# Splitting the last group of queries of an attention kernel in two, with a seventh buffer of exponentials

## The chip, the cores and the metric

The kernel runs on one core of one Trainium2 chip. The metric is device time in microseconds (us), lower is better. The kernel before takes 885.8 us (median of 3 runs, 884.97 to 886.49); the profiled execution has a span of 884.1 us from the first instruction to the last.

The engines are called by the names that the profile uses: PE (matrix multiply), PEld (its weight loads), DVE (vector), ACT (scalar: exponentials and other activations), POOL (GpSimd), SP (the engine that issues transfers).

## The reference

One sequence of 2048 tokens, width 640, 32 heads of 20. An attention branch and a gated branch share one layer norm.

```python
x = A_x                                   # (1, 2048, 640) bf16
xn = layernorm(x)
qkv = (xn @ wqkv) ...                     # 32 heads of 20
scores = einsum("bhqd,bhkd->bhqk", q, k) * 20 ** -0.5
p = softmax(scores)                       # 32 x 2048 x 2048 exponentials
s = einsum("bhqk,bhkd->bhqd", p, v) ... @ wo
# second branch: layernorm, w1, gelu, shifts by 1 or 2 tokens, w2, residual,
#                layernorm, w3, gelu, w4, residual
g = silu(B(xn, w1, w2, w3, w4))
out = x + s * g
```

## The kernel before

The kernel lays out its own schedule when it is built: it lists tasks with their reads, writes, buffers and wished times (`DUE`), orders them for each engine, and emits them with semaphores. Each engine then carries out its list in order. So a change in a constant of the configuration reorders work everywhere.

The 32 heads are taken four at a time (a *quad*, 8 of them), and the queries 512 at a time (4 of them): 32 *groups*. In a group the 2048 keys are 16 tiles of 128. The usual step for a key tile computes the scores of two heads (two PSUM banks, 128 keys x 1024) and one exponential over them on ACT, so a tile costs two exponentials.

```python
    def score_act(self, b, qc, kt, a, gb=None):
        ...
        hs, sa = self.stile()                       # two PSUM banks
        def fn(e):
            for jj in range(2):                     # two heads
                out = self.bank(hs.slot + jj)
                ...
                for c in range(4):
                    ins = e.matmul(out[32 * c:32 * c + 32, :], self.KT[:, b, 128 * kt + 32 * c:...],
                                   self.QM[:, gb, 2 * a + jj, :], start=True, stop=True, tile_position=(0, 32 * c))   # L1420
        T("pe", ..., acq=("S", hs))
        return self.exp_act(hs, sa)

    def exp_act(self, hs, sa):                      # L1444
        self.T("act", ..., lambda e: e.activation(self.PT[:, hp.slot, :],
               self.psum[:, 512 * hs.slot:512 * hs.slot + 1024], AF.Exp, scale=cfg.scale),
               ..., acq=("PT", hp), rel=hs)
```

`PT` holds the exponentials until PE has multiplied them with the values (L1345): six buffers of 128 x 1024. The products gather in PSUM bank 7 (`PVB`), one bank for all groups.

Part of the exponentials is made on DVE from the bits of an integer. A *block* is two key tiles; of each, two heads go to ACT and two to DVE, so a block costs two exponentials on ACT in place of four. `ND[quad][qc]` is the number of blocks of a group. DVE takes the scores to 16-bit integers (L1471, one for each of the two tiles) and makes four pieces of them (L1371, shared by two blocks where a unit has two); PE multiplies each piece with the values (L1380). The scores of a block need two pairs of banks at once:

```python
            pairs = [(0, [0, 1]), (0, [2, 3])]
            high = [(0, [4, 5]), (0, [5, 6]), (1, [4, 6])]
            pl.kind("W", "B", [(0, [4]), (0, [6]), (1, [5])])          # all other matmuls
            pl.kind("S", "B", pairs + ...)                             # scores for ACT
            pl.kind("SD", "B", [(r + q, x + y) for r, x in pairs for q, y in high]     # scores of a block
                    + ([(3, pairs[0][1] + pairs[1][1]), ...] if self.cfg.FALL else []))
```

At the end of a group DVE empties bank 7 (`normalise`). In the last quad it transposes in blocks of 32 (L1493), takes reciprocals (L1495), multiplies (L1501) and transposes back (L1503) into `On7`. In the last group of all, four tiles of 128 tokens then follow: PE multiplies `On7` with the last rows of `wo` (L1602, two banks of kind S), DVE multiplies with the gate (L1609) and adds the part made earlier (L1650), and the row tile is stored (L1652).

```python
    def finish_qc(self, qc):
        split = qc == cfg.NQC - 1
        ...
        for nl in range(4):
            n = 4 * qc + nl
            sl = n % 2
            if split:
                addend, adda = Sb[:, nl, :], [A("Sb", nl, 0), A("Sb", nl, 1)]
            ...
            if split:
                self.wo_last(n, SB2[:, sl, :], ...)                    # L1602, L1609
            ...
            T("dve", ..., lambda e, ...: e.tensor_tensor(OS[:, sl, :], SB2[:, sl, :], addend, op=ALU.add), ...)    # L1650
            T("sp", C_SP, lambda e, ...: e.dma_start(outv[:, n, :], OS[:, sl, :]), ...)                             # L1652
```

Before the first exponential the kernel loads x, normalises it on DVE, ACT and POOL (`POOLN` names the tiles that POOL scales), transposes it on PE and copies it out of PSUM on DVE or ACT, and projects keys and queries of the first quad. A bound on the scores needs the largest key (L1158, L1164, L1166).

## Time and profile before

| what | value | how to read it |
|---|---|---|
| median time | 885.8 us | three runs, 884.97 to 886.49 |
| span of the profile | 884.1 us | one execution |
| first exponential starts | 35.65 us | timeline of ACT |
| last exponential ends | 873.05 us | started 872.00, 1.05 us long |
| ACT busy | 846.9 us, 96% | overlapping instructions included |
| PE busy | 822.8 us, 93% | matmuls are pipelined, so this is not PE at its peak |
| DVE busy | 716.2 us, 81% | |
| POOL busy | 42.9 us, 5% | nearly all in the first 40 us |
| mean granted PE clock | 0.995 | |

A group of the profile is a line of the kernel with its engine, operation, tile and shape; "idle before" is the time its engine stood still just before these instructions, with the instruction that ended most of it. In a timeline a row can stand for several instructions run one after another, as its count says.

### The profile page before, as it was taken

The page shows a single profiled execution, that of the slowest core. Times are in us where ns is not written, and L with a number is a line of the kernel's source. Part 1 is how long each engine was busy: PE and PEld are TensorE (multiplying, and loading weights), DVE is VectorE, ACT ScalarE, POOL GpSimd, SP SyncE. Part 2 cuts the span into 40 slices and gives each one's busy share as a digit, 9 for nine tenths or more (in the row PEclk, how much of TensorE's full clock was granted, in tenths as well). Part 3 has the DMA queues.
Part 4 walks back from the last instruction along what each step waited for, and adds up shares of the span by engine and source line. Part 5 has one row for each costly group of instructions (what it writes and reads, how often), then busy time and mean ns, then how long its engine had stood idle before and what let it go on. Part 6 is the DMA issues. An engine that isn't in the chain of part 4 may idle for free.

```text
span 884.1 us, 34138 instructions
## 1 busy us (share of the span) xinstructions
PE 822.8 (93%) x15594; PEld 361.9 (41%) x15594; DVE 716.2 (81%) x986; ACT 846.9 (96%) x896; POOL 42.9 (5%) x74
## 2 busy tenths in 40 slices
PE   3899999998999999999999899999999799999996
PEld 2433333333444443433334444443433344444553
DVE  7747797876888889999998657997889794898675
ACT  7799999998999999999999999999999999999994
POOL 9500000000000000000000000000000000010000
PEclk9999999999999999999999999999999999999998
DMA  6002632331210002332122302132221212023322
GB/s 224 10 8 61 137 96 73 95 95 36 52 41 25 26 25 64 90 101 52 47 55 62 113 26 56 54 91 69 56 64 44 70 32 69 24 65 101 114 69 75
DMA packets 86481, 59.01 MB, mean 67 GB/s; under 512 B 53057, under 2 KB 77841, under 8 KB 86337
## 3 DMA queue, kind: packets, MB, share of 16 engines
q1 hardware_dynamic: 86336, 56.82, 23.5%
q8 instruction: 123, 2.02, 0.9%
q14 instruction: 22, 0.17, 0.1%
HBM read 42.10 MB, written 10.63 MB: 60 GB/s over the span
## 4 chain that ended last, share of the span: by engine, by line
ACT 55%; PE 19%; DVE 17%; DMA 5%; POOL 1%; issue 1%; POOLq 0%
ACT arena L1444 53%; PE psum L782 8%; PE psum L1420 6%; DVE arena L1371 5%; DVE arena L1471 4%; DMA arena<-recips 3%; PE psum L1345 2%; PE psum L1388 2%; DMA recips<-arena 2%; PE psum L1380 1%; ACT arena L1809 1%; DVE arena L984 1%; ACT arena L1825 1%; DVE arena L1805 1%; DVE arena L1225 1%
## 5 line engine op out<-in xcount | busy, mean ns | idle before, releaser
L1444 ACT ACTIVATE arena<-psum 128x1024 bf16<-128x1024 f32 x834 | 777.8, 1038 | 14.4 <-PE psum L1420 5.0
L1420 PE MATMUL psum<-arena 128*32 128x512 bf16 x4928 | 375.7, 381 | 8.0 <-ACT arena L1444 6.6
L782 PE MATMUL psum<-arena 128*32 128x320 bf16 (+1 forms) x5952 | 359.8, 333 | 6.8 <-DVE arena L1179 2.8
L1471 DVE TENSOR_SCALAR arena<-psum 128x1024 uint16<-128x1024 f32 (+1 forms) x192 | 231.5, 1206 | 42.1 <-PE psum L1388 41.3
L1371 DVE TENSOR_SCALAR arena<-arena 128x4096 uint16<-128x4096 uint16 (+1 forms) x224 | 231.4, 1059 | 3.6 <-PE psum L1380 2.5
L782 PEld LDWEIGHTS psum<-arena 128*32 128x32 bf16 x5952 | 150.5, 97 | 146.2 <-issue 20.7
L1345 PE MATMUL psum<-arena 128*22 128x512 bf16 x1668 | 161.8, 381 | 1.2 <-DVE arena L1506 0.6
L1420 PEld LDWEIGHTS psum<-arena 128*32 128x32 bf16 x4928 | 104.4, 95 | 137.2 <-ACT arena L1444 95.2
L1380 PE MATMUL psum<-arena 128*22 128x512 bf16 x1520 | 126.5, 380 | 2.5 <-DVE arena L1371 2.2
L1388 PE MATMUL psum<-arena 32*128 32x512 bf16 x816 | 85.4, 384 | 16.6 <-ACT arena L1444 9.7
L1345 PEld LDWEIGHTS psum<-arena 128*22 128x22 bf16 x1668 | 42.5, 92 | 55.8 <-issue 11.8
L1388 PEld LDWEIGHTS psum<-arena 32*128 32x128 bf16 x816 | 21.9, 90 | 102.5 <-ACT arena L1444 81.4
L1380 PEld LDWEIGHTS psum<-arena 128*22 128x22 bf16 x1520 | 35.8, 91 | 44.5 <-issue 9.7
L1805 DVE CAST arena<-psum 128x512 bf16<-128x512 f32 x48 | 32.8, 684 | 8.3 <-PE psum L782 8.1
L1225 DVE CAST arena<-psum 128x512 bf16<-128x512 f32 x40 | 27.3, 682 | 10.9 <-PE psum L782 10.8
L1820 DVE TENSOR_TENSOR arena<-psum,arena 128x320 bf16<-128x320 f32 x32 | 15.6, 486 | 22.0 <-PE psum L782 22.0
L1590 DVE SCALAR_TENSOR_TENSOR arena<-psum,arena 128x320 bf16<-128x320 f32 x32 | 15.6, 489 | 19.0 <-PE psum L782 18.9
L1519 DVE TENSOR_TENSOR arena<-arena 128x512 bf16<-128x512 f32 x28 | 19.2, 686 | 11.5 <-DMA arena<-recips 11.4
L984 DVE BATCH_NORM_STATS2 arena<-arena 128x6 f32<-128x320 bf16 x52 | 23.0, 480 | 2.2 <-DMA arena<-in_A_x_dram 2.2
L1286 DVE CAST arena<-psum 128x320 bf16<-128x320 f32 x32 | 15.4, 488 | 10.9 <-PE psum L782 10.5
L1506 DVE COPY arena<-psum 128x512 f32<-128x512 f32 x28 | 19.2, 685 | 3.5 <-PE psum L1345 2.3
L1089 PE MATMUL psum<-arena 128*32 128x128 bf16 x320 | 8.9, 248 | 13.7 <-DVE arena L999 13.1
(103 smaller groups left out, 283.8 us busy)
## 6 DMA issues: line engine op xcount, KB each, us to landing
arena<-in_B_w_dram SPq DMA_DIRECT2D x48, 160.0 KB, 2.6
arena<-recips SPq DMA_DIRECT2D x28, 256.0 KB
arena<-arena SPq DMA_DIRECT2D x124, 32.0 KB, 1.9
arena<-in_B_w_dram SPq DMA_DIRECT2D x4, 960.0 KB, 6.0
arena<-in_A_x_dram SPq DMA_DIRECT2D x8, 320.0 KB, 5.3
arena<-in_A_x_dram SPq DMA_DIRECT2D x16, 160.0 KB, 2.3
out_dram<-arena SPq DMA_DIRECT2D x16, 160.0 KB, 1.8
heads<-arena SPq DMA_DIRECT2D x112, 20.0 KB
```

The costliest lines, as they stand in the source:

```text
L782: ins = e.matmul(pb[32 * c:32 * c + 32, 0:N], lhsT(k, c), rhs(k, c), start=(k == 0), stop=(stop and k == nk - 1), tile_position=(0, 32 * c))
L984: lambda e, li=li, n=n, hh=hh: e.bn_stats(st[:, li, 6 * hh:6 * hh + 6], xn[:, n, hD * hh:hD * hh + hD]),
L1225: T("dve", c_dve(512), lambda e, h=h, c=c: e.tensor_copy(KS[:, 512 * c:512 * c + 512], self.wbank(h)[:, 0:512]), reads=[wa], writes=[A("KS ...
L1345: ins = e.matmul(pb[32 * i:32 * i + 22, 0:512], VA[:, ql, kts[x // 2], i, :], PT[:, slots[x // 2][0].slot, 512 * (x % 2):512 * (x % 2) + 512],
L1371: T("dve", c_dve(w, "4x"), lambda e, v=v, dst=dst: e.tensor_scalar(dst, U[:, ub, 0:w], 0.5, EXP_B[v], op0=ALU.mult, op1=ALU.add), reads=ha ...
L1380: ins = e.matmul(pb[32 * i:32 * i + 22, 0:512], wv, dst[:, at:at + 512].bitcast(BF16), start=first, stop=final, tile_position=(0, 32 * i))
L1388: return e.matmul(out, self.KT[32 * i:32 * i + 32, b, 128 * kt:128 * kt + 128], self.QT[32 * i:32 * i + 32, b, 512 * qc:512 * qc + 512], s ...
L1420: ins = e.matmul(out[32 * c:32 * c + 32, :], self.KT[:, b, 128 * kt + 32 * c:128 * kt + 32 * c + 32], self.QM[:, gb, 2 * a + jj, :], start ...
L1444: lambda e: e.activation(self.PT[:, hp.slot, :], self.psum[:, 512 * hs.slot:512 * hs.slot + 1024], AF.Exp, scale=cfg.scale),
L1471: ins = e.tensor_scalar(U[:, ub, 1024 * at + 512 * k:1024 * at + 512 * k + w], self.psum[:, 512 * hd.slots[k]:512 * hd.slots[k] + w], a_ex ...
L1506: T("dve", c_dve(512), lambda e: e.tensor_copy(Ob[:, :], self.bank(self.PVB)[:, :]), writes=[("PV", 0), A("Ob")], name=f"ob{quad}_{qc}", c ...
L1805: T("dve", c_dve(512), lambda e, h=h, fc=fc, i=i: e.tensor_copy(GT[:, i, fc, :], self.wbank(h)[:, 0:512]), reads=[wa], writes=at, name=f"g ...
```

## The change

The last group of queries (quad 7, queries 1536 to 2047) is done in two halves of 256 queries. A score tile then holds four heads by 256 queries, and one exponential covers all four heads of a key tile. Each half gathers its products in a bank of kind W of its own, and is normalised on its own, so the first half can go on to the output projection while the second is being computed. Four of the 32 tile-halves go to DVE whole (`LAST`: three in the first half, one in the second), with the scores in a pair of kind S. `PT` has seven buffers in place of six. The last outputs are added in place, so the second pair of tiles doesn't wait for the store of the first. With this comes a new set of the tuned constants: `DUE`, `ND`, `RESERVE`, `POOLN`, `TRA` (which transposed tiles ACT copies out), and `FALL` is off. An unused path (`score_half`, `ROWK`) goes.

```diff
-        self.RESERVE = 1000.0
-        self.POOLN = [1, 9, 13, 15]
+        self.RESERVE = 200.0
+        self.POOLN = [1, 5, 9, 13]
...
-        self.FALL = True
+        self.FALL = False
...
+        self.LNA = [3, 3]
+        self.TRA = [1, 5, 7, 9, 11, 13, 15, 17, 19]
+        self.ONP = 0
+        self.LAST = [[[0, 2], [7, 1]], [[2, 1]]]
         self.ND = (
-            [1, 2, 3, 3],
-            [3, 3, 3, 4],
-            [3, 3, 3, 3],
-            [2, 3, 4, 4],
-            [4, 2, 2, 4],
-            [4, 3, 3, 3],
-            [4, 4, 2, 3],
-            [4, 3, 1, 2])
+            [1, 2, 4, 3],
+            [2, 3, 3, 4],
+            [3, 4, 3, 2],
+            [3, 2, 4, 4],
+            [3, 2, 3, 3],
+            [4, 3, 4, 3],
+            [4, 4, 3, 3],
+            [4, 4, 3, 0])
...
-            pl.pool("PT", 6)
+            pl.pool("PT", 7)
...
-                act = bk % 2 == 1
+                act = bk in cfg.TRA
...
+            if last and qc == NQC - 1:
+                for half in range(2):
+                    self.last_half(quad, qc, half, gb)
+                self.finish_qc(qc)
+                continue
...
+    def last_half(self, quad, qc, half, gb):
...
+        mine = cfg.LAST[half]
+        nd = sum(n for _, n in mine)
+        kd = list(range(1, 2 * nd, 2))
+        ks = [k for k in range(cfg.NT) if k not in kd]
...
+        def scores(kt, kind):
+            hs, sa = self.stile()
+            def fn(e):
+                for i in range(4):
+                    o = 256 * (i % 2)
+                    for c in range(4):
+                        ins = e.matmul(self.bank(hs.slot + i // 2)[32 * c:32 * c + 32, o:o + 256], self.KT[:, b, 128 * kt + 32 * c:128 * kt + 32 * c + 32],
+                                       self.QM[:, gb, i, 256 * half:256 * half + 256], start=True, stop=True, tile_position=(0, 32 * c))
+                return ins
+            T("pe", 450, fn, ..., cls=-1, acq=("S", hs))
...
+        for x, kt in enumerate(ks):
+            hs, sa = scores(kt, "a")
+            hp, pa = self.exp_act(hs, sa)
...
+                for m, kx in enumerate(unit):
+                    hs, sa = scores(kx, "d")
+                    T("dve", c_dve(1024),
+                      lambda e, ...: e.tensor_scalar(U[:, ub, 1024 * m:1024 * m + 1024], self.psum[:, 512 * hs.slot:512 * hs.slot + 1024], ...),
+                      ..., rel=hs, cls=-1 - half, ...)
+                for v in range(4):
+                    T("dve", c_dve(w, "4x"), lambda e, ...: e.tensor_scalar(SS[:, k, 0:w], U[:, ub, 0:w], 0.5, EXP_B[v], ...), ...)
...
+        T("dve", c_dve(256), lambda e: e.transpose(Ob[:, c0:c0 + 256], self.wbank(hb)[:, 0:256]), ..., rel=hb)
+        T("dve", c_dve(8, "recip"), lambda e: e.reciprocal(RZ[:, 0, h8:h8 + 8], Ob[:, c0 + 20:c0 + 256:32]), ...)
+        T("dve", c_dve(256, "1x"), fnn, ...)
+        T("dve", c_dve(256, "1x"), lambda e: e.transpose(self.On7[:, 512 * qc + c0:512 * qc + c0 + 256], OnT), ...)
...
-            T("dve", ..., lambda e, sl=sl, addend=addend: e.tensor_tensor(OS[:, sl, :], SB2[:, sl, :], addend, op=ALU.add), ...)
-            T("sp", C_SP, lambda e, sl=sl, n=n: e.dma_start(outv[:, n, :], OS[:, sl, :]), ...)
+            res, resa = (addend, adda) if split else (OS[:, sl, :], [A("OS", sl)])
+            T("dve", ..., lambda e, sl=sl, addend=addend, res=res: e.tensor_tensor(res, SB2[:, sl, :], addend, op=ALU.add),
+              ..., cls=-2 if split and nl > 1 else 0)
+            T("sp", C_SP, lambda e, res=res, n=n: e.dma_start(outv[:, n, :], res), ...)
...
-        self.RR = self.alloc("RR", [7, 512], FP32)
+        self.RR = self.alloc("RR", [6, 512], FP32)
```

## The prediction

> **What bounds the kernel now.** I read the engines' totals first, then the costliest groups of ACT and DVE, then who waits on ACT, and last the timelines of the first 36 us, of the longest stalls and of the end.
>
> ```profile
> PE 822.8 (93%) x15594; PEld 361.9 (41%) x15594; DVE 716.2 (81%) x986; ACT 846.9 (96%) x896; POOL 42.9 (5%) x74
> ACT 55%; PE 19%; DVE 17%; DMA 5%; POOL 1%; issue 1%; POOLq 0%
> L1444 ACT ACTIVATE arena<-psum 128x1024 bf16<-128x1024 f32 x834 | 777.8, 1038 | 14.4 <-PE psum L1420 5.0
> ```
>
> ACT is the bound: 96% busy, the most of the ended-last chain, and 834 of its instructions are the exponentials. From the first (35.65 us) to the end of the last (873.05) there are 837.4 us, in which ACT stands still for 14.4. In steady runs one follows the other faster than its 1038 ns say: 87 in a row take 80.54 us, so the step is (80.54 - 1.04) / 86 = 0.924 us. That is the price of one exponential. PE's 93% overstates it: a set of four 512-column matmuls is issued every 0.21 us though each is drawn 0.38 long.
>
> Then the waits of ACT over the span:
>
> ```profile
> ACT arena L1444 <- PE psum L1420: 5.0, 13, 0.7
> ACT arena L1444 <- PE psum L1345: 4.8, 6, 1.8
> ACT arena L1444 <- PE psum L1388: 3.3, 5, 2.2
> ```
>
> L1420 and L1388 are scores that came late, L1345 a product with the values that had to free a buffer of exponentials. The two long ones of that kind are at 452.7 (1.79 us) and 567.2 (1.65 us). In both, DVE takes an integer conversion (1.22) or the product with reciprocals (0.68) before it empties bank 7, PE waits for the bank, and all six buffers fill. The 2.2 us wait is at 209.6: DVE stood 2.86 us for the transfer of the reciprocals at 207.2, and PE then ran at a granted clock of 0.66 from 210 to 215, which gave another 1.5 us of waits.
>
> The end, in the timeline:
>
> ```profile
> 873.13 0.39 PE L1345 MATMUL psum<-arena 128*22 128x512 bf16 x4
> 874.00 0.72 DVE L1493 STREAM_TRANSPOSE arena<-psum 128x512 f32<-128x512 f32 x1 [0.49 <-PE psum L1380]
> 874.75 0.25 DVE L1495 RECIPROCAL arena<-arena 128x16 f32<-128x16 f32 x1
> 875.04 0.69 DVE L1501 TENSOR_TENSOR arena<-arena 128x512 bf16<-128x512 f32 x1
> 875.77 0.71 DVE L1503 STREAM_TRANSPOSE arena<-arena 128x512 bf16<-128x512 bf16 x1
> 877.04 1.56 DVE L1609 SCALAR_TENSOR_TENSOR arena<-psum,arena 128x640 bf16<-128x640 f32 x2 [0.56 <-PE psum L1602]
> 878.52 0.88 DVE L1650 TENSOR_TENSOR arena<-arena 128x640 bf16<-128x640 bf16 x2
> 879.32 1.55 DVE L1609 SCALAR_TENSOR_TENSOR arena<-psum,arena 128x640 bf16<-128x640 f32 x2
> 880.92 0.96 DVE L1650 TENSOR_TENSOR arena<-arena 128x640 bf16<-128x640 bf16 x2
> ```
>
> After the last exponential: 0.95 us until DVE has the sum, 2.48 of normalising, 0.56 for PE, 4.84 of DVE on four row tiles without a gap, 2.24 for the last store. Sum 11.07.
>
> **What the skill says.** "ScalarE: Activation LUTs", section "What ACT_TABLE_LOAD costs", gives an activation with immediate operands 186 ns + 0.833 ns per element, and an overlap of about 93 ns: estimates of 1039 ns for 1024 elements and 946 for the step. The trace has 1038 and 924. So it is the elements that cost, and four heads by 256 queries cost what two heads by 512 do: the halves alone save ACT nothing. "VectorE: DVE Perf Modes", section "Mode 2×_2P", says PSUM has one read port for DVE; the trace agrees: 1218 ns for 1024 values out of PSUM (L1471), 1221 ns for 4096 16-bit values from the arena (L1371). "SBUF — State Buffer", section "🔬 SBUF: two separate sides", says that DVE (in two-port modes) and POOL lock one pair of ports for a whole instruction; the trace shows L1166 on 4 values per partition taking 2.15 us at 31.72, beside a POOL fill (L951) from 31.69 to 33.84, and it lies ahead of the first exponential.
>
> **The change, part by part.**
>
> *Fewer exponentials on ACT.* A group without blocks has 32, each block takes away 2. `ND` before sums to 95: 32 x 32 - 190 = 834, as the profile counts. After, the 31 ordinary groups have 97 blocks: 31 x 32 - 194 = 798. The last has 32 tile-halves less 4 on DVE: 28, as before (32 - 2 x 2). Together 826, 8 fewer: 8 x 0.924 = **-7.4 us**.
>
> *What DVE takes on.* The ordinary groups go from 93 to 97 blocks, so L1471 from 190 conversions to 198 with the last group's four: +8 x 1.22 = 9.7 us. Pieces: before 156 of 4096 and 68 of 2048. From `ND`, a group with 2 blocks has one double unit, with 3 a double and a single, with 4 two doubles: after, 41 doubles and 15 singles, 164 x 1.221 + 60 x 0.687 = 241.4 us, and the last group adds 4 of 2048 and 8 of 1024 (0.42, from L1191), 6.1. Against 231.4 that is +16. DVE goes to some 742 us, 85% of the span: still beside ACT, but between 340 and 440 us it is already 96% busy. PE is relieved: a block takes away four score sets (4 x 0.43) and a product (0.21), and adds two row-tiled score sets and four products (6 x 0.21), 0.65 us less each.
>
> *Seventh buffer.* Each long wait for L1345 can shrink by one exponential, 0.92 us, and short ones go: of 4.8 us about **-2.5**. Off-path at other times. The cluster at 209.6 may come again elsewhere, as the new order has as many reciprocal transfers; the added DVE work adds waits. I put +0.5 on the rest: together **-2**.
>
> *Last group.* Here I expect a loss. A pair of kind S is written and read in turns: the scores at 867.70 start 0.14 after the exponential that began at 866.52 ended, last 0.60, and their exponential starts at 868.38. One turn is 1.86 us, two pairs give one exponential in 0.93, with under 0.1 us to spare. A tile-half for DVE now sits in such a pair for 0.60 + about 0.1 + 1.22 + about 0.2 = 2.1 us. In that time the other pair gives 2.1 / 1.86 = 1.13 exponentials and two would have given 2.27: 1.14 x 0.924 = 1.05 us lost for an exponential of 0.92 saved. Before, the DVE half of a block sat in banks 4 to 6 and the last 22 exponentials ran without a wait. So the four tile-halves cost 4 x 1.05 = **+4.2 us** that the count of 28 hides. The projection of the first half's tiles needs a pair too; scores come first by class, so it comes when they run out: **+0.3**. The wait for bank 7 at the start of the group (0.36) goes, as the halves have their own banks.
>
> *End.* Normalising 256 columns: DVE took 0.685 for 512 and 0.487 for 320 columns, 1.03 ns per column and 0.157 fixed, so 0.42 for each of three and about 0.2 for the reciprocals: 1.46 in place of 2.48, -1.0. The first half's two tiles (2 x 0.78 + 2 x 0.48 = 2.5 us of DVE) move ahead of the end, but not fully, since they wait for a free pair: -1.6. In DVE's unbroken chain no wait for a store shows, so adding in place brings 0. **-2.6**, a tail of some 8.5 us.
>
> *Head.* Tile 15 is scaled by ACT in place of POOL (two POOL scalings end at 26.7, and the last transposes and keys follow), and POOL, one late job lighter, can let go of L1166 sooner: **-0.8**. The eviction that goes from ACT to DVE is 0.6 us of an ACT that waits there anyway: 0.
>
> Sum: -7.4 - 2 + 4.2 + 0.3 - 0.4 - 2.6 - 0.8 = -8.7. From 885.8: **877 us**, a gain of 1.0%.
>
> **Rivals.**
>
> *The exponentials go and ACT waits instead.* DVE at 85% with transfers in its list, `FALL` off (a block's scores may no longer take all four ACT banks, so they wait for the high ones, which gather the other branches' matmuls) and a `RESERVE` of 200 in place of 1000. For it: all 14.4 us of waits now come from late scores and DVE order. Against: `DUE` moves the second gelu and what follows earlier (603 to 498), out of the quad that gets three more blocks, and DVE had 20 to 25% free in most stretches of 100 us. It would give back 4 to 8: 881 to 885.
>
> *The last group's pair is no loss.* The conversions are placed up to three steps ahead, and the first two fall where the group begins. Then -4: 873. Add a collision of L1166 that vanishes (2 us) and no cluster like that at 210 (4 us): 868 to 870, close to 2%.
>
> *All is in the end.* If the constants only shuffle, what is left is the 2.6 of the end less the 4.2 of the pair: 886 to 888. Against it: the count of exponentials is fixed by the code, and ACT has 96%.
>
> **Range and chances.** The 7.4 is sure as work on ACT, the tail good to 1.5 us, the last group to 2.5, the waits, set by an order I can't see, to 4 or 5. Together about 5 either way: 870.5 to 883.5. Two per cent below is 868.1, which needs waits nearly gone and no loss in the last group: 0.06. Two per cent above (903.5) needs ACT to lose 26 us: 0.03. Within: 0.91.
>
> **What would show it.** 826 exponentials at 1038 ns; ACT busy near 839 us; waits for L1345 below 3 us in all; in the last 27 us gaps before exponentials of about 1 us beside each of four L1471-like conversions; 8 to 9 us from the last exponential to the end; a first exponential at 34 to 35.5. The prediction fails if ACT's waits between first and last exponential exceed 25 us or fall below 6, or if DVE shows stretches of 99% with late conversions.

## The result, and the profile after

The changed kernel takes 890.83 us (median of 6 executions, 888.05 to 894.13); the kernel before, timed beside it, 885.4 (884.59 to 888.73). The ratio is 1.0057, with a 95% interval of 1.003 to 1.0084: 5.4 us slower, where 8.7 us faster was predicted. Timed once more on another occasion (the run `same_again` below) it took 894.05, with executions from 890.77 to 898.35.

The totals by engine, the chain that ended last and the group of the exponentials, from the page of the changed kernel (span 886.3 us; this is its fastest execution, 888.05):

```profile
PE 824.2 (93%) x15946; PEld 370.6 (42%) x15946; DVE 733.2 (83%) x1010; ACT 840.4 (95%) x887; POOL 42.7 (5%) x75
ACT 54%; PE 22%; DVE 13%; DMA 9%; issue 1%; POOL 1%; SPq 0%; DVEq 0%
L1526 ACT ACTIVATE arena<-psum 128x1024 bf16<-128x1024 f32 x826 | 770.7, 1035 | 18.6 <-PE psum L1502 11.0
```

The work went away as intended: 826 exponentials, and 6.5 us less of busy ACT (846.9 before). DVE took on 17. Yet the span grew, and in the chain transfers now have 9% instead of 5.

The waits of ACT in the same execution (waits in all, how many, the longest; L1502 are the two-head scores, L1390 the scores of the new last group, L1349 the products with the values, which free exponential buffers):

```profile
ACT arena L1526 <- PE psum L1502: 11.0, 11, 3.0
ACT arena L1526 <- PE psum L1390: 2.6, 4, 0.7
ACT arena L1526 <- PE psum L1349: 2.1, 5, 1.0
```

The products are down from 4.8 to 2.1, as expected of a seventh buffer. The two-head scores are up from 5.0 to 11.0.

I cut the span at the first exponential's start and the last one's end. Between them lies ACT's own work plus its waits; all columns are microseconds from one profiled execution.

| profiled execution | exps | to the first | first to last | of it ACT waits | after the last | span |
|---|---|---|---|---|---|---|
| before | 834 | 35.65 | 837.41 | 12.64 | 11.04 | 884.1 |
| changed | 826 | 39.09 | 834.84 | 17.19 | 12.37 | 886.3 |
| changed, `same_again` | 826 | 38.10 | 844.14 | 25.91 | 12.36 | 894.6 |

Without its waits the middle is 824.77 before and 817.65 (818.23) after. So in the first profile of the change the account is +3.4 head, -7.1 exponentials, +4.3 waits in the last group (4.65 against 0.36), +0.3 other waits, +1.3 end: together +2.2. In the second it is +2.5, -6.5, +4.3, +9.0, +1.3: together +10.5. The median lies between. Four things are to be explained: head, end, last group, and waits that differ from one execution to the next.

**The end.** The last exponential ended at 873.94. From the timeline after it (start, duration, engine, line):

```profile
873.27 0.49 DVE L1676 SCALAR_TENSOR_TENSOR arena<-psum,arena 128x320 bf16<-128x320 f32 x1 [0.74 <-PE psum L785]
...
875.93 0.49 DVE L1676 SCALAR_TENSOR_TENSOR arena<-psum,arena 128x320 bf16<-128x320 f32 x1 [0.32 <-PE psum L785]
...
877.07 0.42 DVE L1426 TENSOR_SCALAR arena<-arena 128x1024 uint16<-128x1024 uint16 x1
...
878.94 0.44 DVE L1441 STREAM_TRANSPOSE arena<-psum 128x256 f32<-128x256 f32 x1
...
881.64 1.56 DVE L1695 SCALAR_TENSOR_TENSOR arena<-psum,arena 128x640 bf16<-128x640 f32 x2 [0.83 <-PE psum L1688]
883.11 0.88 DVE L1737 TENSOR_TENSOR arena<-arena 128x640 bf16<-128x640 bf16 x2
```

From the transpose of the second half (878.94) the rest is short, as predicted. But the transpose comes 5.0 us after the last exponential, against 0.95 before. Ahead of it DVE evicts projections of the 512 queries of the group *before* (L1676), and a piece of the last group (L1426) stands behind them at 877.07, though the last conversion that such pieces are made of began at 859.85.

**The last group.** ACT's timeline of the changed kernel:

```profile
843.83 1.02 ACT L1526 ACTIVATE arena<-psum 128x1024 bf16<-128x1024 f32 x1 [1.99 <-PE psum L1502]
845.59 5.62 ACT L1526 ACTIVATE arena<-psum 128x1024 bf16<-128x1024 f32 x6 [0.74 <-PE psum L1390]
851.94 1.02 ACT L1526 ACTIVATE arena<-psum 128x1024 bf16<-128x1024 f32 x1 [0.73 <-PE psum L1390]
853.41 6.52 ACT L1526 ACTIVATE arena<-psum 128x1024 bf16<-128x1024 f32 x7 [0.45 <-PE psum L1390]
860.66 3.08 ACT L1526 ACTIVATE arena<-psum 128x1024 bf16<-128x1024 f32 x3 [0.74 <-PE psum L1390]
```

Five waits, 1.99 + 0.74 + 0.73 + 0.45 + 0.74 = 4.65 us. They stand beside the four tile-halves that DVE converts out of a pair of banks:

```profile
841.88 1.22 DVE L1419 TENSOR_SCALAR arena<-psum 128x1024 uint16<-128x1024 f32 x1
843.81 1.22 DVE L1419 TENSOR_SCALAR arena<-psum 128x1024 uint16<-128x1024 f32 x1
851.46 1.22 DVE L1419 TENSOR_SCALAR arena<-psum 128x1024 uint16<-128x1024 f32 x1
859.85 1.23 DVE L1419 TENSOR_SCALAR arena<-psum 128x1024 uint16<-128x1024 f32 x1 [0.22 <-PE psum L1390]
```

The longest, 1.99, lies ahead of the last exponential of the group before (28 follow it), as the first two conversions are placed early and hold both pairs. Before, the same stretch had one wait of 0.36.

**The head.** The changed kernel around its first exponential (L1771 is a small step of the layer norms, L955 a fill of POOL, L1166 ACT's eviction of projected keys, L1171 the key bound, which was L1166 in the kernel before):

```profile
30.30 2.20 DVE L1771 TENSOR_SCALAR arena<-arena 128x16 f32<-128x16 f32 x1
30.33 2.14 POOL L955 MEMSET arena<- 128x2048 bf16 x1
...
36.45 0.78 ACT L1166 ACTIVATE arena<-psum,arena 128x512 bf16<-128x512 f32 x1 [1.01 <-DVE arena L1163]
...
37.01 0.24 DVE L1171 TENSOR_SCALAR arena<-arena 128x4 bf16<-128x4 f32 x1
...
39.09 1.02 ACT L1526 ACTIVATE arena<-psum 128x1024 bf16<-128x1024 f32 x1 [0.48 <-PE psum L1484]
```

The key bound is free of POOL's fill now, 0.24 us instead of 2.15, as I had hoped. The fill hits another small DVE instruction instead, L1771: 2.20 us for 16 values a partition. That agrees with the Trainium skill, "SBUF — State Buffer", section "🔬 SBUF: two separate sides" (one of the two locks the other out for a whole instruction). And the last projected keys come later: ACT evicts them at 36.45, against 31.53 before. Eleven evictions of projected values by DVE lie ahead of the first exponential; in the kernel before there are seven.

### The profile page after: what moved, and what is told of

Its sections match the earlier page's. It is cut to its first block, busy times and chain, and to the rows that moved or that the text cites. A ratio compares the mean times of both kernels' runs of the same rounds, so it can differ in the third digit from the quotient of the medians.

```text
span 886.3 us, 34862 instructions
## 1 busy us (share of the span) xinstructions
PE 824.2 (93%) x15946; PEld 370.6 (42%) x15946; DVE 733.2 (83%) x1010; ACT 840.4 (95%) x887; POOL 42.7 (5%) x75
## 3 DMA queue, kind: packets, MB, share of 16 engines
q1 hardware_dynamic: 86336, 56.82, 23.2%
## 4 chain that ended last, share of the span: by engine, by line
ACT 54%; PE 22%; DVE 13%; DMA 9%; issue 1%; POOL 1%; SPq 0%; DVEq 0%
ACT arena L1526 50%; PE psum L785 8%; PE psum L1502 6%; DMA arena<-recips 4%; DVE arena L1467 4%; DVE arena L1553 4%; ACT arena L1896 2%; DMA recips<-arena 2%; PE psum L1349 2%; DMA arena<-in_B_w_dram 2%; PE psum L1390 2%; PE psum L1476 1%; PE psum L1484 1%; ACT arena L1825 1%; DMA queries<-arena 1%
## 5 line engine op out<-in xcount | busy, mean ns | idle before, releaser
L1502 PE MATMUL psum<-arena 128*32 128x512 bf16 x4608 | 349.8, 380 | 6.0 <-ACT arena L1526 4.2
L1553 DVE TENSOR_SCALAR arena<-psum 128x1024 uint16<-128x1024 f32 x195 | 236.4, 1213 | 43.3 <-PE psum L1484 42.7
L1467 DVE TENSOR_SCALAR arena<-arena 128x4096 uint16<-128x4096 uint16 (+1 forms) x224 | 235.8, 1078 | 1.6 <-PE psum L1476 0.7
L785 PEld LDWEIGHTS psum<-arena 128*32 128x32 bf16 x5952 | 149.0, 97 | 143.0 <-issue 26.2
L1349 PE MATMUL psum<-arena 128*22 128x512 bf16 x1596 | 152.4, 380 | 1.3 <-DVE arena L1588 0.8
L1502 PEld LDWEIGHTS psum<-arena 128*32 128x32 bf16 x4608 | 99.3, 95 | 129.5 <-ACT arena L1526 93.0
L1476 PE MATMUL psum<-arena 128*22 128x512 bf16 x1552 | 127.4, 380 | 2.4 <-DVE arena L1467 2.2
L1349 PEld LDWEIGHTS psum<-arena 128*22 128x22 bf16 x1596 | 39.8, 92 | 52.9 <-issue 12.0
L1476 PEld LDWEIGHTS psum<-arena 128*22 128x22 bf16 x1552 | 36.7, 92 | 46.0 <-issue 9.1
L1676 DVE SCALAR_TENSOR_TENSOR arena<-psum,arena 128x320 bf16<-128x320 f32 x32 | 15.3, 484 | 9.3 <-PE psum L785 9.2
L1094 PE MATMUL psum<-arena 128*32 128x128 bf16 x320 | 9.4, 249 | 13.6 <-DVE arena L1003 10.5
L1896 ACT ACTIVATE arena<-arena 128x12288 bf16<-128x12288 bf16 x2 | 20.9, 10444 | 0.0
```

The lines of the kernel that those rows point to most:

```text
L785: ins = e.matmul(pb[32 * c:32 * c + 32, 0:N], lhsT(k, c), rhs(k, c), start=(k == 0), stop=(stop and k == nk - 1), tile_position=(0, 32 * c))
L1349: ins = e.matmul(pb[32 * i:32 * i + 22, 0:512], VA[:, ql, kts[i // 2], i, :], PT[:, slots[i // 2][0].slot, 512 * (i % 2):512 * (i % 2) + 512],
L1467: T("dve", c_dve(w, "4x"), lambda e, v=v, dst=dst: e.tensor_scalar(dst, U[:, ub, 0:w], 0.5, EXP_B[v], op0=ALU.mult, op1=ALU.add), reads=ha ...
L1476: ins = e.matmul(pb[32 * i:32 * i + 22, 0:512], wv, dst[:, at:at + 512].bitcast(BF16), start=first, stop=final, tile_position=(0, 32 * i))
L1553: ins = e.tensor_scalar(U[:, ub, 1024 * at + 512 * k:1024 * at + 512 * k + w], self.psum[:, 512 * hd.slots[k]:512 * hd.slots[k] + w], a_ex ...
L1896: T("act", 2750 + c_act(2 * FC * 512), lambda e: e.activation(GT[:, :, :, :], GT[:, :, :, :], AF.Gelu_apprx_tanh), reads=gta, writes=gta, ...
```

## The experiments

All are compared with runs of the kernel before on the same occasion (885.89 to 886.93 us), except where an absolute reading of a profile is meant.

### The changed kernel once more, and the halves alone

`same_again` is the changed kernel without an edit.

> The changed kernel a second time, for a second profile. Theory A (order: the time went into a later first exponential, into the last group and into the end, and all three are fixed by the order of work): first exponential again at 39.1 us within 0.3, last exponential to end 12.4 within 0.5, median 889 to 892. Theory B (transfers: the changed order leaves DVE waiting for transfers whose landing varies): the extra over 888 us shows as longer DVE waits for the reciprocals, 2 us or more above the 17 us of the first profile, and the first exponential may move by 1 us.

Measured: 894.05 us, ratio 1.0094 (1.0061 to 1.0126). The loss is there again, and larger. The tail is the same (12.36), the head moved by a microsecond (38.10), and DVE's waits for reciprocals differ, as theory B had it. They were, in the first profile and in this one:

```profile
DVE arena L1601 <- DMA arena<-recips: 17.0, 12, 3.0
DVE arena L1602 <- DMA arena<-recips: 21.9, 13, 3.5
```

In the second profile, the longest stall of ACT (timeline; "idle before" in brackets with what ended it):

```profile
562.29 0.69 DVE L1602 TENSOR_TENSOR arena<-arena 128x512 bf16<-128x512 f32 x1 [3.48 <-DMA arena<-recips]
...
562.96 0.61 PE L786 MATMUL psum<-arena 128*32 128x512 bf16 x8 [3.76 <-DMA arena<-in_B_w_dram]
...
564.15 1.02 ACT L1527 ACTIVATE arena<-psum 128x1024 bf16<-128x1024 f32 x1 [3.84 <-PE psum L1503]
...
564.71 1.10 PE L1503 MATMUL psum<-arena 128*32 128x512 bf16 x8
```

DVE stands 3.48 us for the reciprocals, whose load was issued at 556.16, and PE 3.76 us for weights whose two loads were issued behind it at 556.79. Both engines work through a fixed list, so the scores that ACT needs, ready to be computed, stand behind. Then PE runs slowly: eight score matmuls last 1.10 us instead of 0.60. The stretches of this execution (from:to, length, busy time and count of PE, PEld, DVE, ACT and POOL, PE clock, DMA share, GB/s):

```profile
555.00:558.00 3.00, 3.00 (x60) 1.21 (x56) 2.95 (x4) 3.00 (x4) 0.00 (x0) 1.00 0.04 2
558.00:562.90 4.90, 1.20 (x24) 0.30 (x12) 1.42 (x3) 2.31 (x3) 0.00 (x0) 1.00 0.50 119
...
564.30:566.60 2.30, 2.30 (x24) 0.76 (x17) 0.00 (x0) 1.62 (x2) 0.00 (x0) 0.50 0.10 26
```

A clock of 1.00, then a standing PE, then 0.50. "TensorE: Matmul & The Clock Gate" in the Trainium skill, section "🔬 Part 1: The HAM clock gate (the "warmup" mystery)", says that PE falls to half its rate after about 3.4 us of idleness and needs about 3.4 us of work to come back; the 3.76 us and the 0.50 fit it. But a shorter stand than the page's was enough elsewhere. In the kernel before PE stood 2.43 us, and its clock from 211 to 213 was 0.50:

```profile
209.18 0.40 PE L1388 MATMUL psum<-arena 32*128 32x512 bf16 x4 [2.43 <-DVE arena L1471]
...
211.00:213.00 2.00, 2.00 (x24) 0.79 (x20) 1.18 (x2) 1.10 (x2) 0.00 (x0) 0.50 0.00 0
```

In the first profile of the changed kernel a stand of 2.99 us (ended at 89.57) was followed by a clock of 1.00. So here the length of one stand doesn't settle it. At 564 a late transfer cost ACT more than its own wait: 3.84 us, and then 0.68, 0.39 and 0.17 by 568.5.

`halves_alone` is the kernel before with the split last group and the outputs added in place; six buffers and all constants as before, 834 exponentials.

```diff
 # the changed kernel, with what follows put back to the kernel before
-            pl.pool("PT", 7)
+            pl.pool("PT", 6)
-        self.free("ones_bf", "ones_f", "m1", "e4", "maskn6")
-        self.RR = self.alloc("RR", [6, 512], FP32)
+        self.RR = self.alloc("RR", [7, 512], FP32)
 # ... and DUE, RESERVE, POOLN, FALL, TRA and ND
```

> The kernel before with the last group in two halves and the last outputs in place, and nothing else: constants, six buffers and blocks as before, 834 exponentials. Theory A: first exponential at 35.65 as before; waits of 4 to 5 us before exponentials of the last group, where the score pairs hold tile-halves for DVE (before: 0.4); end after the last exponential 8 to 9 us if only the normalising counts, 12 if the leftover output tiles of the group before hold it as in the changed kernel. Total 886 to 890. Rival (the halves are a gain and the constants ate it): 882 to 884.

Measured: 888.12 us, ratio 1.0021 (1.001 to 1.0032). To the first exponential 36.45, waits 16.84 of which 3.33 in the last group, and 8.68 us after the last exponential. So the halves do bring 11.04 - 8.68 = 2.4 us at the end, and the last group gives back 3.33 - 0.36 = 3.0.

### The last group and the end

`no_dve_in_last`: the changed kernel with no tile-half of the last group on DVE (830 exponentials).

```diff
-        self.LAST = [[[0, 2], [7, 1]], [[2, 1]]]
+        self.LAST = [[], []]
```

> The changed kernel with no tile-half of the last group on DVE: all 32 are exponentials on ACT, 830 in all. Theory A: the 4.6 us of waits around the last group go and 4 exponentials (3.7 us) come, so the last exponential ends within 1.5 us of the changed kernel's 873.9; the second half's pieces no longer hold the end, so from the last exponential to the end 1 to 3 us less than 12.4; total 1 to 4 us below the changed kernel. Rival (a tile-half on DVE saves its exponential): 3 to 4 us above.

Measured: 892.58 us, ratio 1.0073 (1.0046 to 1.0101). No wait is left in the last group, and four more exponentials stand in it: 4 x 0.924 = 3.7 us in place of 4.65. Putting halves of tiles on DVE there gains nothing that the times show. I had expected the end to get 1 to 3 us shorter, but it is 12.65, so it is not the last group's pieces on DVE that hold it.

`old_last_group`: the changed kernel with the last group in one part of 512 (826 exponentials).

```diff
-            if last and qc == NQC - 1:        # the two halves
+            if False:
-            [4, 4, 3, 0])
+            [4, 4, 3, 2])
```

> The changed kernel with the last group as before: one part of 512 queries, two blocks, one bank of sums; new constants, seven buffers and the rest as changed, 826 exponentials. Theory A: waits around the last group fall from 4.6 to under 1 us, so the last exponential ends near 869 to 870; the end after it 13 to 15 us, as the leftover output tiles of the group before are still there and all four last tiles follow the normalising; total 1 to 4 us below the changed kernel. Rival (the halves are a gain): 2 to 4 us above.

Measured: 893.14 us, ratio 1.0078 (1.005 to 1.0105). No waits are left in the last group, but ACT's waits in all are 17.24 us as with the halves (17.19), so the last exponential ends at 873.1 and not at the 869 to 870 that I expected. And 16.78 us follow it, where the same last group in the kernel before leaves 11.04. The new order is worse at the end by 5.7 us, and the halves win 16.78 - 12.37 = 4.4 of them back.

`without_group_before`: the outputs of the group before the last (512 of the 2048 rows) are left out, and those rows of the output are not written.

```diff
             if last:
+            if last and qc != 2:
                 self.finish_qc(qc)
```

> The changed kernel with the outputs of the last-but-one group of 512 queries left out (their transposes, projection matmuls, adds and stores are gone, so 512 rows of the output are not written). Theory (what the new order leaves of that group lies behind the last exponential and the second half's output waits for it): from the last exponential to the end 8.4 to 9.2 us, as in the kernel with only the new last group (8.68), against 12.37 of the changed kernel. Rival (the halves' own chain is longer in the new order, for instance because the second half's row-tiled scores and reciprocals stand later): it stays above 11.5 us. The last exponential itself may end up to 2 us earlier or later, which says nothing.

Measured: one execution, 887.01 us. The last exponential ended at 876.86, and the end is

```profile
877.35 0.44 DVE L1441 STREAM_TRANSPOSE arena<-psum 128x256 f32<-128x256 f32 x1
...
880.62 1.56 DVE L1695 SCALAR_TENSOR_TENSOR arena<-psum,arena 128x640 bf16<-128x640 f32 x2 [0.56 <-PE psum L1688]
882.09 0.89 DVE L1737 TENSOR_TENSOR arena<-arena 128x640 bf16<-128x640 bf16 x2
```

The transpose follows 0.49 us after the last exponential, and the tail is 8.44 us. So the 12.37 of the changed kernel is the group before, left over; the halves' own chain is as short as in `halves_alone`.

### The head

`value_projection_later`: the wished times of the first value projection as in the kernel before, nothing else.

```diff
-            ... v0=-32.0, v0s=-0.97, ...
+            ... v0=-24.5, v0s=-0.38, ...
```

> The changed kernel with the two wished times of the first value projections as before (-24.5 and -0.38 in place of -32.0 and -0.97). All later work is ordered anew too, so only the first exponential is read. Theory H (the head is late because 11 value evictions of DVE, with their matmuls, stand ahead of the first exponential, where there were 7): about 3 stand ahead of it now, and it starts at 36 to 37.5 us, not 38 to 39. Rival (the tiles scaled by POOL, or the reused small buffers, make it late): it stays at 38 or later.

Measured: one execution, 892.58 us. Three value evictions are now ahead of the first exponential, which starts here (timeline, changed constant):

```profile
36.02 4.69 ACT L1526 ACTIVATE arena<-psum 128x1024 bf16<-128x1024 f32 x5 [0.48 <-PE psum L1484]
```

The head is back within 0.4 us of before, so in this order the earlier value projection had set it. But the time doesn't follow: the order that results has 25.06 us of waits, among them 3.67 at 67.6 and 2.24 at 72.6. The head was mended and something else broke.

### The waits for reciprocals

`later_multiply` moves each of the 28 DVE multiplications with reciprocals, and the store behind it, up to 2.5 us later in its engine's list, after the order is made; `before_later_multiply` does the same to the kernel before.

```diff
+            self.put_later(2500.0, None)
+        for t in sorted((t for t in tasks if t.name.startswith("on") ... and t.eng == "dve"), ...):
+            move(t, t.start + wait)           # not past a task on the same engine that needs it
```

> The changed kernel with its order as it is, but for one thing: DVE's multiplication with the reciprocals (28 of them) stands up to 2.5 us later in DVE's list, or just ahead of the next use of its buffers, and the four stores of its result with it. No work is added or left out. Theory B2 (in the changed order DVE comes to that multiplication before the reciprocals have landed, and all behind it waits: evictions, then PE, then scores): DVE's waits for the reciprocals fall from 17 to 23 us to under 8, the waits of 2.8 to 3.8 us near 90 and 564 us go, and with them the stretches of half PE clock behind them; waits before 835 us fall from 12 to 21 to 8 to 11, time 885 to 889, and the spread between runs shrinks. Theory A2 (the waits come from more work on DVE, the transfer is only what it is seen waiting for): less than 2 us gained, as DVE still has the same work in the same stretches.

> The kernel before with the same shift of the 28 multiplications by up to 2.5 us. Theory B2: DVE's waits for the reciprocals fall from 11.4 us to under 5, the wait of 2.2 us at 210 us and the half clock behind it go, time 881 to 884 against 886. Theory A2: within 1 us of the kernel before.

DVE's waits for reciprocals fell from 17.0 and 21.9 us (two profiles of the changed kernel) to

```profile
DVE arena L1631 <- DMA arena<-recips: 1.9, 2, 1.3
```

and the changed kernel took 889.03 us (ratio 1.0036, 1.0021 to 1.0051; executions 886.96 to 892.8, 17 of them) where it had had 890.83 and 894.05; the interval lies below that of `same_again` and overlaps that of the first timing. Its profiled middle is 834.14 long, with 16.24 us of waits. The stall at 564 is missing, but the first profile of the changed kernel has no such stall either, and there the middle was 834.84 with 17.19 us of waits: 15 us less of DVE's waits took 1 us off ACT's, and the wait of 3.0 us near 90, which theory B2 expected to go, stayed. So late reciprocals may be part of the loss and of its scatter; that they are isn't shown. On the kernel before, both theories failed: 889.43 us, ratio 1.0037 (1.0021 to 1.0053), 3.5 us worse. Its waits for reciprocals vanished, and others came, one of 3.03 us at 497.9 and one of 1.54 at 622.7.

### The buffers, and the order itself

By now two edits had mended what they aimed at and lost it elsewhere. `small_buffers_freed` is the kernel before with only the early release:

```diff
+        self.free("ones_bf", "ones_f", "m1", "e4", "maskn6")
```

> The kernel before with the five small buffers of constants given back early, as the changed kernel does to make room, and nothing else. The memory they held is used again by the layer norm's small buffers, which so wait for POOL and DVE work on the constants. Theory H2: the first exponential about 1 us later than 35.7 to 36.5, the rest of the span as before (time 886 to 888). Rival: no difference in the head, within 0.3 us.

Measured: one execution, 885.82 us, first exponential at 37.12: no loss in time, and 1.5 us in the head, where two executions of the changed kernel differ by 1.0.

`old_constants` is all of the changed code with the constants of before (834 exponentials).

```diff
 # the changed kernel; DUE, RESERVE, POOLN, FALL, TRA and ND as before
-            k0=-80.6, k1=-174.4, ... v0=-32.0, v0s=-0.97, v1=8.6, ...
+            k0=100.3, k1=-164.3, ... v0=-24.5, v0s=-0.38, v1=48.3, ...
```

> All of the changed code (halves, seven exponential buffers, six reciprocal buffers, early release, outputs added in place) with the order's constants of the kernel before (due times, conversions per group of heads, which tiles GpSimd and ScalarE take): 834 exponentials. Theory (the new constants carry the loss, and the code itself is near neutral): first exponential at 35.5 to 37.2 us, last exponential to end 8.4 to 9.2 us, time 884 to 889 us, so 2 to 8 us below the changed kernel. Rival (the code carries the loss, through another use of the buffers): first exponential after 38 us or a tail of 12 us or more, and 890 us or more.

Measured: 892.99 us, ratio 1.0066 (1.0044 to 1.0088). My theory fails, and its rival is right on the time and wrong on the way: the head is 37.15 and the tail 9.77, both better than in the changed kernel. The middle is 843.68, with 16.57 us of waits before exponentials and 2.69 before a gate activation. So the loss doesn't need the new constants.

Then the buffers of the change alone on the kernel before, and the row buffer alone:

```diff
 # seventh_buffer_alone: both pairs and the release; six_row_buffers: only the second pair
-            pl.pool("PT", 6)
+            pl.pool("PT", 7)
-        self.RR = self.alloc("RR", [7, 512], FP32)
+        self.RR = self.alloc("RR", [6, 512], FP32)
```

> The kernel before with the buffers of the change alone: seven exponential buffers, six buffers of output rows, five small constant tiles released early; last group, constants of the order and outputs as before (834 exponentials). Theory A (the buffers are near neutral, and the 4.9 us by which the whole code with the old constants lies above the halves alone come from the halves and the buffers being laid out together): 885 to 888 us, waits outside the last group 10 to 13 us, first exponential 35.6 to 37.2 us. Theory B (the seventh buffer itself costs, because the order uses it to let the exponentials run further ahead of the products, so that the rest of the work meets later transfers): 889 to 892 us, with waits outside the last group above 14 us or a first exponential above 37.5 us.

> The kernel before with six instead of seven buffers for the first residual rows, and nothing else. Theory A (one row buffer fewer is not felt): 885 to 887 us and the tail after the last exponential 10.8 to 11.3 us. Theory B (the missing row buffer delays the outputs at the end and the row loads): tail 12 us or more, 888 us or more.

Measured: 891.8 us with the seven buffers (1.007, 1.0054 to 1.0086), 890.16 with six row buffers alone (1.0051, 1.0032 to 1.007). With seven buffers the waits before exponentials fall to 11.21 us, as a seventh buffer promises, but the head is 38.67, the tail 13.75, and a gate activation waits 2.69. This late head has only seven value evictions ahead of it, so more of them are not the only way to one. With one row buffer fewer, head (35.52) and tail (11.23) stay, and ACT's waits grow in the middle:

```profile
ACT arena L1444 <- PE psum L1388: 6.7, 6, 2.7
ACT arena L1444 <- PE psum L1345: 6.6, 7, 1.8
ACT arena L1444 <- PE psum L1420: 6.4, 10, 3.9
```

against 3.3, 4.8 and 5.0 before. Neither of the two theories fits that. These rows (`RR`, layer norm factors) serve only the first projection of the gated branch, and are free before its gelu at 226 us; but ACT's waits after the gelu grew too, from 7.7 to 11.8 us (before it from 5.0 to 7.5). The edit has also given the builder's order a new course from early on: matmuls of the first 30 us stand otherwise. So I measured what a new order costs when nothing else is changed. `order_nudged_a`, `_b` and `_c` are the kernel before with one wished time moved by 1 to 3:

```diff
-            ... u2=-21.8 ...
+            ... u2=-20.8 ...      # a
-            ... v1=48.3 ...
+            ... v1=51.3 ...       # b
-            ... v1s=-24.33 ...
+            ... v1s=-23.33 ...    # c
```

> A control: the kernel before with one due time of its order changed by one step's unit (u2 from -21.8 to -20.8) and nothing else; the same buffers, last group and 834 exponentials, only the order of the small pieces of work differs from about a quarter of the run on. Theory A (any new layout of the order loses the fitting of the old one, whatever the reason for it): 2 to 6 us above the kernel before, by waits outside the last group of 14 to 20 us instead of 12.3. Theory B (the row buffer itself costs the 4.2 us of the six-row-buffers kernel): within 1.5 us of the kernel before.

> The same control with another due time (v1 from 48.3 to 51.3); the order differs from about 40 per cent of the run on. Theory A: 2 to 6 us above the kernel before. Theory B: within 1.5 us of it.

> The same control with a third (v1s from -24.33 to -23.33); the order differs almost from its start. Theory A: 2 to 6 us above the kernel before, with the first exponential between 35 and 38 us. Theory B: within 1.5 us of it.

| kernel | median us | ratio to before, 95% | to the first | first to last | after the last |
|---|---|---|---|---|---|
| before (same occasion) | 886.93 | | | | |
| nudged a | 894.08 | 1.0075 (1.005 to 1.0101) | 35.66 | 844.58 | 11.06 |
| nudged b | 895.31 | 1.0086 (1.006 to 1.0112) | 35.59 | 844.40 | 10.91 |
| nudged c | 910.12 | 1.0273 (1.024 to 1.0306) | 35.68 | 858.99 | 13.23 |

The loss was expected, its size not: 7.2, 8.4 and 23.2 us, for orders that nobody would call different in kind. The waits are not where I put them, either: before exponentials a has only 13.09 us; its new ones are before the gate activation (L1825), where the kernel before has none. In c the first gelu (L1738) alone waits 8.2 us, and exponentials wait 14.1 us for products (a: 7.5, b: 9.4, before: 4.8). From a, then from c:

```profile
ACT arena L1825 <- DVE arena L1820: 6.0, 3, 3.3
...
ACT arena L1444 <- PE psum L1345: 14.1, 9, 3.1
ACT arena L1738 <- DVE arena L1734: 8.2, 1, 8.2
```

### Two attempts at a better kernel

Both have six exponential buffers and constants chosen anew, so that work that needs a transfer stands later than the landings seen in the traces; `retuned_old_end` keeps the last group in one part (834 exponentials), `retuned_halves` splits it (831).

```diff
-            k0=100.3, ... v1=48.3, ... w1=675.4, ... st=56.8, ...
+            k0=75.21, ... v1=55.93, ... w1=734.29, ... st=5.42, ...      # retuned_old_end; also RESERVE, POOLN, TRA, ND
-        self.HALF = True          # a switch for the split, added
+        self.HALF = False
```

> An attempt at a better kernel: the old last group in one part of 512 with its outputs added in place, six exponential buffers, 834 exponentials, and constants of the order chosen anew so that the multiplications, the query projection and the weight loads stand later than their transfers in the traces (6 us for the load of the reciprocals, 6.5 us for the store of the keys). Theory (waits for late transfers are what can still be saved: 12 to 13 us of waits outside the last group in the order of before): waits outside the last group 8 to 11 us, time 882 to 885 us, 1 to 4 us under the kernel before. Rival (other waits take their place, as when only the multiplications of the kernel before were moved): 886 to 892 us.

> The same with the last group in two halves of 256 (831 exponentials, six buffers, five tile-halves converted on VectorE in the last group). Theory: waits outside the last group 8 to 11 us, 4 us of waits in the last group, 8.4 to 9.5 us from the last exponential to the end, time 881 to 886 us. Rival (other waits take their place): 886 to 892 us.

Measured: 887.65 us (1.0004, 0.9991 to 1.0018) and 889.2 (1.0028, 1.0017 to 1.0038). The first is level with the kernel before: head 35.15, waits 11.54, tail 10.55, a little better in each, in a profile of its fastest execution (884.74). The second has the good tail (8.46) and 20.72 us of waits, 18.0 of them outside the last group, where I had expected 8 to 11. Neither beats the kernel before; both times lie in the rival's range.

## Why the prediction was wrong

It predicted a gain of 8.7 us, and there was a loss of 5.4. Three steps failed: the sum of the waits outside the last group (-2), the head (-0.8) and the end (-2.6). All three had been worked out in the order of the kernel before.

- **The count (-7.4) was right.** 826 exponentials, and 7.1 and 6.5 us less of ACT's own work in the two profiles. DVE ended at 733.2, not 742.
- **The last group (+4.2) was right,** in size and in mechanism: 4.3 us more waits beside the tile-halves that DVE takes from a pair (3.0 in `halves_alone`), and none without them (`no_dve_in_last`).
- **The seventh buffer (-2.5) agrees as a term:** the waits for products fell from 4.8 to 2.1, though alone (`seventh_buffer_alone`) only to 3.7, and a nudge of the order moves them with six buffers to 7.5 to 14.1. What failed is the sum it stood in, "together -2" for all waits outside the last group. They came out at +0.3 in one profile and +9.0 in the other. I had let +0.5 stand for everything that a new order does. Shown in its place: a new order alone adds 6.4 us of ACT's waits in nudge a and 22.1 in c (19.08 and 34.78 between first and last exponential, against 12.64). What the waits of this order come from is seen in part: DVE and PE stand in their lists for transfers (17.0 and 21.9 us for reciprocals, against 11.4), and PE can fall to half clock after it.
- **The head (-0.8) had the wrong sign:** +2.5 to +3.4. The two effects that I named are small next to one that I passed over. `v0` and `v0s` were among the changed wished times, and four more evictions of values, with their matmuls, moved ahead of the first exponential; with the old values it is back at 36.02. Another build had a late head without them (38.67, `seventh_buffer_alone`). The collision of POOL and DVE left the key bound, as I had said, and took another instruction.
- **The end (-2.6) had its mechanism right and met something else:** the halves shorten it by 2.4 (`halves_alone`) and by 4.4 in the new order. But the new order leaves outputs of the group before for after the last exponential, 3.9 us (12.37 against 8.44 without them). I had worked the end out in the old order and carried it over.

The rivals were nearer, and still too low. "The exponentials go and ACT waits instead" named late transfers in DVE's list, and gave 881 to 885; "all is in the end" gave 886 to 888. The range was too narrow at its upper end: "the waits, set by an order I can't see, to 4 or 5" was too small for what an order does. In the first profile the head (4.2 off) and the end (3.9 off) missed by more than the waits outside the last group (2.3 off); in the second the waits missed by most (11.0). Of the signs that I had named, the 826 exponentials, ACT busy near 839 (840.4), the waits for products and the gaps of the last group came true; the first exponential and the tail did not, and the second profile has more than 25 us of waits. The nudged orders, with the same instructions for ACT, differ from the kernel before by 7 to 23 us, nearly all of it between the first and the last exponential.

That limits what can be said of the parts. Each edit of a buffer or a constant makes another order, so a run with one part undone differs in that part and in the order. Terms that can be read locally in a profile (count, last group, tail, the group before, the value projection) are shown. That the buffers or constants are bad in themselves is not shown: the whole code with old constants (1.0066) and with its own (1.0057) lie within each other's intervals, and the kernel before is among the best orders that I ran: of the fourteen other builds timed more than once beside it none is faster by its interval. Three nudges say that an order can easily be worse; they don't say how a typical one is. Why the old order is so good, and whether the new code has one as good, stays open.

## What to carry to other kernels

Where a program lays out its own order, every edit is two edits: the one you meant and a new order. Before crediting or blaming a part, run a control that changes only the order (here a wished time by 1), and judge parts by what is local in the profile: the stretch before the first, between the first and the last, and after the last instruction of the bounding engine. And a term worked out in the old order, like the end here, holds in the new one only if what stands around it is still there.

## What the runs showed of the hardware that was not expected

- One late transfer can cost more than itself: 3.76 us of a standing PE were followed by a stretch at a granted clock of 0.50, with eight 512-column matmuls in 1.10 us instead of 0.60. A stand of 2.43 us was followed by one too (the kernel before, 211 to 213 us), one of 2.99 us was not (the changed kernel, 90 to 93 us).
- The load of reciprocals, 256 KB, was usable 6.1 us after its issue (556.16 to 562.29; 4.7 to 6.4 us for the thirteen such loads that DVE waited for in this profile) with weight loads issued behind it, while the core's transfers moved 119 GB/s over the 4.9 us of the stall.
- The lock between POOL and DVE moves rather than goes: 2.15 us on the key bound in one order, 2.20 us on another small instruction in the next, each time as long as POOL's fill (2.15, 2.14).
